# Retention heads and a cosine MLP on one core: the state product moved onto 64x64 quarters of the matmul array

## The chip, the cores and the metric

The kernel runs on one core of a Trainium2 chip. The metric is device time in microseconds (us) of that core, from launch to end; lower is better. The profile shows one execution, instruction by instruction, on the engines PE (matmul; PEld is its weight load), DVE (vector), ACT (scalar), POOL and SP (which only issues transfers).

## The reference

Two stages, one after the other. First a retention recurrence for 4 batches, 8 heads, 768 tokens and head size 64:

```
state = gamma[h] * state + outer(k[t], v[t])
y[t]  = scale * q[t] @ state
```

Then an MLP without bias over the 3072 tokens (model size 512, inner size 2048): `h = x @ w_in; out = (h * cos(h)) @ w_out`, where x is y with its heads side by side.

## The kernel before

**Chunks.** The recurrence is computed in chunks of 128 tokens. A slot is one chunk of two batches (b = 0 and 1), all 8 heads; 6 chunks and two pairs of batches make 12 slots, p = 0 to 11. In each slot PE makes, for each head and batch:

- A = k qᵀ inside the chunk (`a_mm`, L366): the 128 keys lie on PSUM partitions as two halves x = 0 and 1 of 64, and the 128 queries are columns. DVE multiplies A by a triangular mask into `am` (`a_mask`, L372).
- Y, in one PSUM bank for each batch, from three parts: the state times q (L428, in `y1_mm`), and `am` times v for each half of the keys (`intra`, L414). Keys of the second half see only queries of the second half, so there the matmul has 64 columns and not 128.
- S = kᵀ v, added to the running state in the bank `st_ps` (`s_mm`, L460): one matmul of 128 rows, 64 columns of the array and 64 moving columns for each head and batch. A copy of the state, `stb`, is used by the next slot.

The decay is folded into q and v by per-token factors (`gq`, `gk`; `conv_q`, `conv_v`). q and k reach PE transposed in `qkt`: by PE up to slot 5 (`t_mm`), by a DMA transpose from slot 6 on (`dma_t`, issued by SP).

**Quarters.** The 128x128 array can be used as four 64x64 quarters: a row group r (which 64 partitions feed it) and a column group c (which 64 PSUM partitions it writes). A and Y are written for quarters and S for halves of 128x64; everything else uses the whole array. Two row groups must not write one PSUM bank at the same time. Y's two halves of the keys sit on different row groups and go into the same bank, so `y1_mm` first sends each row group to its own bank, then `hop` puts a wait on another engine's queue (SP for p up to 5, POOL after), and `y2_mm` sends each row group to the other bank.

**The MLP** works on groups of two slots (512 tokens), g = 0 to 5: `f_mm` (L472, four matmuls of 512 columns for each of 16 blocks of the inner size), cosine by ACT (`f_cos`, L480), product by DVE (`f_mul`, L484), then `o_mm` (L517, 16 matmuls for each of 4 token blocks). Groups 0 and 1 can also be made in halves of 256 tokens (`h_mm`, L493); `HALF0` says for how many blocks of group 0.

**Order.** Up to slot 5 a planner (`Plan`) with a cost and a rank for every operation decides the order on each engine before the kernel is built; a seed and a jitter of the ranks pick one order among many. Where it finds PE without work early on it adds matmuls on zeros (`idle_mm`, L546). `LOADS` is the order of the big transfers on POOL's queue. From slot 6 on the order is written out: `block(p)` stands once in each 8 steps of the loop, each step being one `f_mm` and one quarter of an `o_mm`; in it stand Y's first part, the hop, A of slot p+1, Y's second part, the copies, and S. After it come the conversions of slot p+2, its two DMA transposes, and the loads of slot p+4, three transfers of 512 KB on SP's queue. The loads of slots 8 and 9 are issued just ahead of this loop.

**PSUM.** One bank of eight holds the state; the other seven go round among all users in the order in which they were given back.

Of the kernel before, what the change touches and what calls it, by code (L numbers as in the profile page):

```python
# [159 lines left out]
            op["fn"](op["eng"])  # L160


SEED, JIT, HOLD = 60, 4.0, "PD"
HALF0, SPARE, RF, RM, COLD = 4, 1, 40.0, 40.0, 5.2


@with_exitstack
def kernel(
# [21 lines left out]
    NB = 3  # L190
    DMA_T = 6

    ORDER = [0, NC] + [x for x in range(1, NP) if x != NC]
    LATE = NC

    scale = 1.0 / math.sqrt(D)
# [34 lines left out]
    cosb = [sb([128, 4 * C], BF16, f"cosb{i}") for i in range(3)]  # L231
    kx = sb([128, H, 2, D], BF16, "kx")
    vx = sb([128, 2, H, D], BF16, "vx")
    mask = sb([128, 128], BF16, "mask")
    zero = sb([128, 256], BF16, "zero")
    lgp = sb([128, NC, H], FP32, "lgp")
    gq = sb([128, NC, H], FP32, "gq")
    gk = sb([128, NC, H], FP32, "gk")


    gtf = gt[1].rearrange("p f t -> p (f t)")
# [23 lines left out]

    def load(eng, p, names):

        bp, c = divmod(ORDER[p], NC)
        for n in names.split():
            t, src = SRC[n[0].lower()]  # L270
            if len(n) == 1:
                t = (qb(p) if n == "Q" else kb(p)) if n in "QK" else t[p % PRE]
                eng.dma_start(  # L273
                    out=t.rearrange("p b h d -> p (b h) d"),
                    in_=src[ds(2 * bp, 2), :, ds(c * C, C), :].rearrange(
                        "b h t d -> t (b h) d"))
            else:
                b = int(n[1])
                eng.dma_start(
                    out=t[p % PRE][:, b],  # L280
                    in_=src[2 * bp + b, :, ds(c * C, C)].rearrange("h t d -> t h d"))
# [27 lines left out]
                             in1=bc(gq, ORDER[p] % NC), op=ALU.mult)  # L309

    def conv_v(p, b, e):
        ENG[e].tensor_tensor(out=vb(p)[:, b], in0=vf[p % PRE][:, b],  # L312
                             in1=bc(gk, ORDER[p] % NC), op=ALU.mult)

# [36 lines left out]
    def kt(n, b, h):  # L351
        return qkt[n][ts(b, 64), 1, h, :]

    def a_mm(p, u):
        n = p % NB
        bk = held["a", p, u] = [banks.take(), banks.take()]
        ap = [t.rearrange("p (a t) -> p a t", a=HP) for t in bk]
        for a in range(HP):
            h = 4 * u + a
            for x in range(1 if p < 2 else 2):  # L360
                for b in range(2):
                    if p < 2:
                        nc.tensor.matmul(ap[b][:, a, :], lhsT=kt(n, b, h), rhs=qt(n, b, h),  # L363
                                         tile_position=(64 * b, 0))
                        continue
                    nc.tensor.matmul(ap[b][ts(x, 64), a, :], lhsT=kt(n, b, h)[:, ts(x, 64)],  # L366
                                     rhs=qt(n, b, h), tile_position=(64 * b, 64 * x),
                                     skip_group_check=True)

    def a_mask(p, b, u):  # L370
        bank = held["a", p, u][b]
        nc.vector.tensor_tensor(  # L372
            out=am[p % 2][b][u], in0=bank.rearrange("p (a t) -> p a t", a=HP),
            in1=(dec[:, b] if p < 2 else mask.unsqueeze(1).to_broadcast([128, HP, 128])),
            op=ALU.mult)
        banks.give(bank)

# [28 lines left out]

    def intra(p, b, a, x, **kw):

        ms = []
        for j in range(2):
            h = 2 * a + j
            ms.append(nc.tensor.matmul(  # L414
                held["yp", p][b][ts(j, 64), a, 64 * x :], lhsT=vs[p % NB][ts(x, 64), b, h, :],
                rhs=am[p % 2][b][h // 4][ts(x, 64), h % 4, 64 * x :],
                start=False, stop=True, tile_position=(64 * x, 64 * j), skip_group_check=True))
        return ms

    def y1_mm(p):  # L420
        bk = [banks.take(), banks.take()]
        held["y", p, 0], held["y", p, 1] = bk
        held["yp", p] = [t.rearrange("p (a t) -> p a t", a=HP) for t in bk]
        for a in range(HP):
            for b in range(2):
                for j in range(2):
                    h = 2 * a + j
                    nc.tensor.matmul(  # L428
                        held["yp", p][b][ts(j, 64), a, :], lhsT=stb[p % 2][ts(b, 64), h, :],
                        rhs=qt(p % NB, b, h), start=(a == 0), stop=False,  # L430
                        tile_position=(64 * b, 64 * j), skip_group_check=True)
        for a in range(HP):
            held["part", p] = intra(p, 1, a, 1) + intra(p, 0, a, 0)

    def hop(p):
        ms = held["part", p]
        held["hop", p] = (nc.sync if p <= 5 else nc.gpsimd).nop(nofuse=True)
        for m in ms:
            after(m, held["hop", p])

    def y2_mm(p):
        for a in range(HP):
            for m in intra(p, 1, a, 0) + intra(p, 0, a, 1):
                if a == 0:
                    after(held["hop", p], m)

    def y_copy(p, b, e):
        bank = held["y", p, b]
        copy(e, xt[(p // 2) % 2][:, :, ts(2 * (p % 2) + b, C)],
             bank.rearrange("p (a t) -> p a t", a=HP))  # L450
        banks.give(bank)

    def has_s(p):
        return p != 1 and (p == LATE or ORDER[p] % NC < NC - 1)

    def s_mm(p):
        x = 1 if p == LATE else p
# [108 lines left out]
        in0=far[:, :8].unsqueeze(2).to_broadcast([128, 8, 16]),  # L566
        in1=far[:, 8:24].unsqueeze(1).to_broadcast([128, 8, 16]), op=ALU.add)
    nc.vector.tensor_scalar(out=ident, in0=dist, scalar1=0.0, scalar2=None, op0=ALU.is_equal)
    nc.vector.tensor_scalar(out=mask, in0=dist, scalar1=0.0, scalar2=None, op0=ALU.is_ge)
    nc.vector.tensor_scalar(out=far, in0=dist, scalar1=0.0, scalar2=1.0e6,  # L570
                            op0=ALU.is_lt, op1=ALU.mult)
    nc.vector.tensor_tensor(out=dist, in0=dist, in1=far, op=ALU.max)
# [9 lines left out]
    for i in range(7):  # L582
# [5 lines left out]
    MERGE = 4  # L588
    CQ, CD = "D", "P"
    SPLIT = {(1, 1, 0), (0, 1, 1)}  # L590
    HM, HCQ, HCV = "q2", "", ""
    plan = Plan({"bank": 7, "cos": 3, "sem": 8, "out": 4, "port": 1, "ring": 7}, 6.5)
    add = plan.add
    SB2 = {"D": (0.33, 0.42), "A": (0.49, 0.585)}
# [3 lines left out]
    prev = None  # L598
    at = lambda tm: dict(start=0.0, free=0.0, done=tm, lat=0.0)
    ld["q", 0, 0], ld["q", 0, 1], ld["k", 0, 0], ld["k", 0, 1] = map(at, (3.9, 5.0, 7.4, 7.4))  # L600
    LOADS = ["Q1", "K1", "v0", "v1", "w0a", "w0b", "w1", "w2", "q2", "k2", "w3a", "v2", "w3b", "o0", "q3", "k3", "v3",
             "o1", "o2", "o3", "q4", "k4", "v4", "q5", "k5", "v5", "q6", "k6", "v6",
             "q7", "k7", "v7"]
    LAG = {"w1": 0.15}
    pend = []
    for i, x in enumerate(LOADS):
# [25 lines left out]
    for p in range(PL + 2):  # L632
# [85 lines left out]
        if p < 2:  # L718
            for b in range(2):
                T["y", p, b] = add("E", 0.24, lambda e, p=p, b=b: y_first(p, b), ym[b], 10 * p + 3,  # L720
                                   [("bank", 1)], (), "col", name="y%d%d" % (p, b))
            if p == 0:
                T["s", p] = add("E", 0.25, lambda e, p=p: s_mm(p), sm, 17, (), (),
                                "col", name="s%d" % p)
        else:

            a_next = MERGE <= p < PL
            def y(e, p=p, a_next=a_next):
                y1_mm(p)
                hop(p)  # L730
                if a_next:
                    a_mm(p + 1, 0)
                    a_mm(p + 1, 1)
                    y2_mm(p)
                if has_s(p):
                    s_mm(p)
                if not a_next:
                    y2_mm(p)
            o = add("E", 0.66 + 0.445 * a_next + (0.35 if a_next else 0.45) * has_s(p), y,
                    ym[0] + ym[1] + sm, 10 * p + 3, [("bank", 6 if a_next else 2)], (), "quad",  # L740
                    name="y%d" % p)
            T["y", p, 0] = T["y", p, 1] = T["s", p] = o
            if a_next:
                T["a", p + 1, 0] = T["a", p + 1, 1] = o
# [56 lines left out]
    plan.run({"S": 2.5, "P": 3.2, "A": 5.5, "D": 3.6, "E": 4.2}, COLD, 0.6, (4.2, 18.0, 0.225, lambda e: idle_mm(e, 2)), HOLD)  # L801
    plan.emit()

    for p in (PL + 2, PL + 3):
        load(nc.sync, p, "q k v")


    def block(p):
        nxt = p + 1 < NP
        y1_mm(p)  # L810
        hop(p)
        if nxt:
            a_mm(p + 1, 0)
            a_mm(p + 1, 1)
        y2_mm(p)
        for b in range(2):
            y_copy(p, b, "A")
        if has_s(p):
            s_mm(p)
            s_copy(p, "D")  # L820
        if nxt:
            for u in range(2):
                for b in range(2):
                    a_mask(p + 1, b, u)
# [11 lines left out]
    for g in range(2, NG + 1):  # L836
        for s in range(16):
            hf, r = divmod(s, 8)
            p = 2 * (g + 1) + hf
            if g < NG:  # L840
                f_mm(g, s)
                f_cos(("f", g, s))
                f_mul(g, s)
            if g == NG and s == 12:
                last_o(NG - 1, 3)
                break
            o_mm(g - 1, *divmod(s, 4))
            if s % 4 == 3:
                o_out(g - 1, s // 4, "A")
            if p < NP and r == 3:  # L850
                block(p)
                if p + 2 < NP:
                    conv(p + 2)
                if p + 4 < NP:
                    load(nc.sync, p + 4, "q k v")
            if s % 4 == 3:
                o_dma(g - 1, s // 4)

# [29 lines left out]
```

## Time and profile before

| | |
|---|---|
| median of 3 runs | 209.99 us (209.96 to 210.13) |
| the profiled execution | 210.4 us, its span 208.5 us |
| PE busy | 203.3 us (97% of the span), 2017 matmuls |
| DVE, ACT, POOL busy | 107.8, 116.1, 80.1 us |
| granted PE clock | 1.0 throughout |
| bytes moved | 32.05 MB, mean 154 GB/s |

The span is the time from the first to the last instruction; 1.9 us of the execution lie outside it. In the page and its views an instruction is named by its line in the kernel, its engine and what it writes from what. A matmul's duration in these views includes its way through the array, so that neighbours overlap: what a matmul costs is read from the distance between starts.

### The profile page before, as it was taken

To read this page: it belongs to the slowest core of one execution; us is meant where nothing else is said; L and a number is where in the kernel's file an instruction comes from. 1 tells how busy PE (TensorE), PEld (TensorE's weight loads), DVE (VectorE), ACT (ScalarE), POOL (GpSimd) and SP (SyncE) were. 2 spreads that over 40 slices of the span, in tenths; PEclk is the share of its full clock that TensorE was granted. 3 is DMA by queue.
4 is the path that set the end of the run, shared out by engine and by line. 5 is a ranking of instruction groups with operands and counts; after the bars stand their busy time and mean duration, and the time that the engine had idled before them with its cause. 6 is when DMAs were issued, how large, how long until landed. Compare 5 with 4: busy or idle time off the path is not lost.

```text
span 208.5 us, 4822 instructions
## 1 busy us (share of the span) xinstructions
PE 203.3 (97%) x2017; PEld 108.9 (52%) x2017; DVE 107.8 (52%) x186; ACT 116.1 (56%) x194; POOL 80.1 (38%) x84
## 2 busy tenths in 40 slices
PE   7999999999999999999999999999999999999993
PEld 2556456889555545455455455454444444444462
DVE  4465888977725647438438438338332334443000
ACT  7777787579655456556556556554545553553120
POOL 8889979999999007007007007000000000000000
PEclk9999999999999999999999999999999999999999
DMA  6999999999999599999994602401101101110222
GB/s 117 183 260 222 309 251 293 209 331 343 343 296 185 149 237 247 211 209 239 227 237 47 176 0 54 150 0 57 50 0 53 50 9 44 50 50 21 80 79 76
DMA packets 57495, 32.05 MB, mean 154 GB/s; under 512 B 46592, under 2 KB 51968, under 8 KB 57472
## 3 DMA queue, kind: packets, MB, share of 16 engines
q0 software_dynamic: 14352, 15.47, 33.6%
q1 hardware_dynamic: 42976, 16.13, 32.0%
q8 instruction: 16, 0.26, 0.5%
q10 hardware_dynamic: 144, 0.13, 0.2%
q14 instruction: 7, 0.06, 0.1%
HBM read 27.26 MB, written 6.29 MB: 161 GB/s over the span
## 4 chain that ended last, share of the span: by engine, by line
PE 91%; DMA 6%; POOL 1%; DVE 0%; ACT 0%; issue 0%; DVEq 0%; POOLq 0%
PE bank L517 38%; PE bank L472 32%; PE bank L493 7%; DMA w_in_sb<-in_moe_w_in_dram 4%; PE bank L366 3%; PE bank L337 2%; PE bank L414 2%; PE st_ps L460 2%; PE bank L537 2%; PE bank L428 2%; DMA qf<-in_q_dram 1%; PE bank L546 1%; POOL am L384 1%; PE bank L363 0%; ACT gt L380 0%; DVE qs L299 0%
## 5 line engine op out<-in xcount | busy, mean ns | idle before, releaser
L480 ACT ACTIVATE cosb<-bank,halfpi 128x512 bf16<-128x512 f32 x96 | 65.6, 690 | 57.3 <-PE bank L472 52.7
L517 PE MATMUL bank<-w_out_sb,gt 128*128 128x512 bf16 x368 | 91.1, 379 | 0.0
L484 DVE TENSOR_TENSOR gt<-bank,cosb 128x512 bf16<-128x512 f32 x76 | 51.7, 689 | 55.3 <-ACT cosb L480 55.3
L472 PE MATMUL bank<-xt,w_in_sb 128*128 128x512 bf16 x304 | 77.0, 379 | 0.1
L517 PEld LDWEIGHTS <-gt 128*128 128x128 bf16 x368 | 35.6, 98 | 42.3
L472 PEld LDWEIGHTS <-w_in_sb 128*128 128x128 bf16 x304 | 28.9, 98 | 34.2 <-DMA w_in_sb<-in_moe_w_in_dram 0.4
L308 POOL TENSOR_TENSOR qs<-qf,gq 128x512 bf16<-128x512 f32 x18 | 18.5, 1045 | 44.8 <-PE bank L414 44.7
L372 DVE TENSOR_TENSOR am<-bank,mask 128x512 bf16<-128x512 f32 x40 | 24.8, 681 | 0.3 <-PE bank L366 0.3
L312 POOL TENSOR_TENSOR vs<-vf,gk 128x512 bf16<-128x512 f32 x22 | 22.7, 1045 | 1.6 <-DMA vf<-in_v_dram 1.4
L297 ACT COPY ob<-bank 128x512 f32<-128x512 f32 (+1 forms) x24 | 13.9, 578 | 15.4 <-PE bank L517 14.2
L493 PE MATMUL bank<-xt,w_in_sb 128*128 128x256 bf16 x160 | 18.8, 273 | 0.0
L297 ACT CAST xt<-bank 128x512 bf16<-128x512 f32 x24 | 12.9, 589 | 9.6 <-PE bank L414 9.0
L501 DVE TENSOR_TENSOR gt<-bank,cosb 128x512 bf16<-128x512 f32 x20 | 13.5, 689 | 8.8 <-ACT cosb L480 8.8
L493 PEld LDWEIGHTS <-w_in_sb 128*128 128x128 bf16 x160 | 15.4, 98 | 2.6
L299 DVE CAST stb<-st_ps 128x512 bf16<-128x512 f32 x10 | 6.9, 690 | 11.3 <-PE st_ps L460 11.1
L546 PE MATMUL bank<-zero 128*128 128x512 bf16 x33 | 10.6, 448 | 1.1 <-DVE halfpi L562 1.1
L297 ACT CAST ks<-kf 128x512 bf16<-128x512 f32 x20 | 11.5, 629 | 0.2 <-DMA kf<-in_k_dram 0.2
L273 POOL DMA_DIRECT2D vf<-in_v_dram x8 | 9.5, 1189 | 0.0
L297 ACT COPY qkt<-bank 128x512 bf16<-128x512 bf16 x13 | 7.1, 594 | 2.7 <-PE bank L337 2.4
L414 PE MATMUL bank<-am,vs 64*64 64x64 bf16 (+1 forms) x320 | 8.3, 205 | 0.1
L299 DVE COPY ob<-bank 128x256 f32<-128x256 f32 x1 | 0.4, 425 | 13.4 <-PE bank L537 13.4
L366 PE MATMUL bank<-qkt 64*64 64x128 bf16 x320 | 7.2, 218 | 0.0
(59 smaller groups left out, 108.8 us busy)
## 6 DMA issues: line engine op xcount, KB each, us to landing
out_dram<-ob SPq DMA_DIRECT2D x23, 256.0 KB, 2.3
vf<-in_v_dram POOLq DMA_DIRECT2D x8, 512.0 KB, 8.4
qf<-in_q_dram POOLq DMA_DIRECT2D x6, 512.0 KB, 10.4
kf<-in_k_dram POOLq DMA_DIRECT2D x6, 512.0 KB, 9.7
w_out_sb<-in_moe_w_out_dram POOLq DMA_DIRECT2D x4, 512.0 KB, 12.8
qf<-in_q_dram SPq DMA_DIRECT2D x4, 512.0 KB, 4.5
kf<-in_k_dram SPq DMA_DIRECT2D x4, 512.0 KB, 6.7
vf<-in_v_dram SPq DMA_DIRECT2D x4, 512.0 KB, 7.5
```

Of the source, the lines that this page charges most:

```text
L297: nc.scalar.copy(out=out, in_=in_)
L308: ENG[e].tensor_tensor(out=qb(p)[:, b], in0=qf[p % PRE][:, b], in1=bc(gq, ORDER[p] % NC), op=ALU.mult)
L312: ENG[e].tensor_tensor(out=vb(p)[:, b], in0=vf[p % PRE][:, b], in1=bc(gk, ORDER[p] % NC), op=ALU.mult)
L366: nc.tensor.matmul(ap[b][ts(x, 64), a, :], lhsT=kt(n, b, h)[:, ts(x, 64)], rhs=qt(n, b, h), tile_position=(64 * b, 64 * x), skip_group_che ...
L372: nc.vector.tensor_tensor(out=am[p % 2][b][u], in0=bank.rearrange("p (a t) -> p a t", a=HP), in1=(dec[:, b] if p < 2 else mask.unsqueeze(1 ...
L472: nc.tensor.matmul(bank, lhsT=w_in_sb[:, i, ts(f, 128)], rhs=xt[g % 2][:, i, :], start=(i == 0), stop=(i == KIN - 1))
L480: nc.scalar.activation(out=cb, in_=bank, func=AF.Sin, bias=halfpi)
L484: nc.vector.tensor_tensor(out=gt[g % 2][:, f, :], in0=bank, in1=cb, op=ALU.mult)
L493: nc.tensor.matmul(bank[:, ts(e, 256)], lhsT=w_in_sb[:, i, ts(f + e, 128)], rhs=xt[g % 2][:, i, ts(hf, 256)], start=(i == 0 and e == 0), s ...
L501: nc.vector.tensor_tensor(out=gt[g % 2][:, f : f + 2, ts(hf, 256)], in0=bank.rearrange("p (f t) -> p f t", f=2), in1=cb.rearrange("p (f t) ...
L517: nc.tensor.matmul(bank, lhsT=gt[g % 2][:, f, ts(j, 128)], rhs=w_out_sb[:, f, :], start=(f == 0), stop=(f == KOUT - 1))
L546: nc.tensor.matmul(bank[:, : 256 * n].rearrange("p (n t) -> p n t", n=n), lhsT=zero[:, :128], rhs=zero.unsqueeze(1).to_broadcast([128, n, ...
```

## The change

1. **S on quarters.** `s_part(p, r)` makes S from the 64 tokens of row group r: 32 matmuls of 64x64 for a slot where there were 16 of 128x64. Both row groups write the bank `st_ps`, so S too gets a hop between its two halves.
2. **One block.** `y_block` makes the lists of all matmuls of a slot for each row group (Y from the state, Y's first part, S's first half on row group 0, A of the next slot, Y's second part, S's second half on row group 1), and `quarters` emits them in one interleaved order, by a small table of when each quarter would be free. `told` places the two hops, on SP for p up to 4 and on POOL after. In slots 2 and 3 A of the next slot stays apart, as before.
3. **Halves swapped.** From slot 8 on (`SWAP`), for the four heads of one half (which half depends on the batch), the first 64 tokens of k and v lie on partitions 64 to 127 and the last 64 on 0 to 63. With that each quarter gets as many matmuls of 64 columns as of 128 in A and Y. It takes a second mask (two more small DVE instructions at the start), a factor table `gk3` with swapped copies (three small transfers on SP's queue after the planned part), and loads of k and v in six pieces each: 13 transfers for a slot instead of 3, with the same bytes in the same 256-byte runs.
4. A's matmul of the second half of the keys now has 64 columns and not 128 (`lo` in `a_one`), since its first 64 columns are masked away in any case.
5. **The planned part** gets another seed, other ranks for cosine and product, `HALF0` 6 for 4 (two more blocks of group 0 made in halves), another order of the loads of k3, v3 and o1, o2, and new costs for the Y blocks.

```diff
-SEED, JIT, HOLD = 60, 4.0, "PD"
-HALF0, SPARE, RF, RM, COLD = 4, 1, 40.0, 40.0, 5.2
+SEED, JIT, HOLD = 59011, 4.0, "PD"
+HALF0, SPARE, RF, RM, COLD = 6, 1, 50.0, 30.0, 5.2
...
+            elif n[1] == "s":
+                fl = t[p % PRE].rearrange("p b h d -> p (b h) d")
+                for x in range(2):
+                    for lo, n4, th in ((0, 4, x), (4, 8, 1 - x), (12, 4, x)):
+                        eng.dma_start(out=fl[ts(x, 64), ds(lo, n4), :],
...
+    def second(p, x, b, u):
+        return x ^ (u ^ b if p >= SWAP else 0)
...
+    def a_one(p, ap, u, a, b, x):
+        h, lo = 4 * u + a, 64 * second(p, x, b, u)
+        return nc.tensor.matmul(
+            ap[b][ts(x, 64), a, lo:], lhsT=kt(p % NB, b, h)[:, ts(x, 64)],
+            rhs=qt(p % NB, b, h)[:, lo:], tile_position=(64 * b, 64 * x), skip_group_check=True)
...
+    def quarters(rows):
+        free = [[0.0, 0.0], [0.0, 0.0]]
+        left = [list(r) for r in rows]
+        while left[0] or left[1]:
+            best = None
+            for r in range(2):
+                for c in range(2):
+                    nxt = next((m for m in left[r] if m[0] == c), None)
+                    if nxt:
+                        t = max(free[r][c], nxt[2])
+                        if best is None or t < best[0]:
+                            best = (t, r, nxt)
+            t, r, m = best
+            left[r].remove(m)
+            free[r][m[0]] = t + m[1] / 2.4
+            m[3]()
...
+    def s_part(p, r):
...
+                    m = nc.tensor.matmul(
+                        st_ps[ts(b, 64), h, :], lhsT=kb(x)[ts(r, 64), b, h, :],
+                        rhs=vb(x)[ts(r, 64), b, h, :],
+                        start=(ORDER[x] % NC == 0 and h == 0 and r == 0), stop=True,
+                        tile_position=(64 * r, 64 * b), skip_group_check=True)
+                    told("s", p, r, m)
...
+        for r in range(2):
+            ms = y_inter(p, r) + y_part(p, r, 0)
+            if has_s(p) and r == 0:
+                ms += s_part(p, 0)
+            if a_next:
+                ms += a_rows(p + 1, r)
+            ms += late(y_part(p, r, 1), t1)
+            if has_s(p) and r == 1:
+                ms += late(s_part(p, 1), t2)
+            rows.append(ms)
+        return quarters(rows)
...
+    for x in range(2):
+        nc.sync.dma_start(out=gk3[ts(x, 64), ds(n, n)], in_=gk3[ts(1 - x, 64), :n])
+    nc.sync.dma_start(out=gk3[:, ds(2 * n, n)], in_=gk3[:, :n])
     for p in (PL + 2, PL + 3):
-        load(nc.sync, p, "q k v")
+        load(nc.sync, p, "q ks vs")
...
     def block(p):
         nxt = p + 1 < NP
-        y1_mm(p)
-        hop(p)
-        if nxt:
-            a_mm(p + 1, 0)
-            a_mm(p + 1, 1)
-        y2_mm(p)
+        y_block(p, nxt)
         for b in range(2):
             y_copy(p, b, "A")
         if has_s(p):
-            s_mm(p)
             s_copy(p, "D")
```

## The prediction

> **What bounds the kernel now.** I read the page first: busy shares, then the chain that ended last.
>
> ```profile
> PE 203.3 (97%) x2017; PEld 108.9 (52%) x2017; DVE 107.8 (52%) x186; ACT 116.1 (56%) x194; POOL 80.1 (38%) x84
> PE 91%; DMA 6%; POOL 1%; DVE 0%; ACT 0%; issue 0%; DVEq 0%; POOLq 0%
> ```
>
> A busy PE is not by itself the bound, but the chain says it is: 91% of the span runs over PE, and no other engine is over 56% busy. The chain in order of time shows from where on:
>
> ```profile
> 11.08 8.57 DMA w_in_sb<-in_moe_w_in_dram
> 19.70 1.04 PE bank L472 x4
> ...
> 92.29 0.86 PE bank L517 x4
> 93.16 0.35 PE bank L428 x16
> ...
> 94.43 0.37 PE st_ps L460 x16
> 94.80 0.97 PE bank L472 x4
> 95.77 0.86 PE bank L517 x4
> ```
>
> PE's last wait for a transfer ends at 19.70 us (weights of the MLP). After it every piece is PE, back to back: four whole-array matmuls take 0.86 us, and 0.97 after a block of small ones. So what the change saves inside PE's blocks after 19.70 us comes off the end one for one, unless a new wait appears. Next, the timeline of PE over one such block (slot 7):
>
> ```profile
> 92.78 0.38 PE L517 MATMUL bank<-w_out_sb,gt 128*128 128x512 bf16 x1
> 93.08 0.42 PE L428 MATMUL bank<-qkt,stb 64*64 64x128 bf16 x16
> 93.33 0.33 PE L414 MATMUL bank<-am,vs 64*64 64x128 bf16 x14
> 93.46 0.22 PE L366 MATMUL bank<-qkt 64*64 64x128 bf16 x2
> 93.50 0.22 PE L414 MATMUL bank<-am,vs 64*64 64x128 bf16 x2
> 93.52 0.69 PE L366 MATMUL bank<-qkt 64*64 64x128 bf16 x30
> 94.00 0.42 PE L414 MATMUL bank<-am,vs 64*64 64x128 bf16 x16
> 94.36 0.44 PE L460 MATMUL st_ps<-vs,ks 128*64 128x64 bf16 x16
> 94.73 0.39 PE L472 MATMUL bank<-xt,w_in_sb 128*128 128x512 bf16 x1
> ```
>
> The first column is the start. From the first small matmul to the next whole-array one is 94.73 - 93.08 = 1.65 us. Read so, the blocks of slots 2 to 11 take 1.51, 1.28, 1.61, 1.62, then 1.65 five times, and 1.09 (slots 2 and 3 hold no A, slot 11 neither A nor S).
>
> **Prices, from the starts one by one in this window.** On one quarter matmuls of 128 columns start 56 ns apart (93.165, 93.221, 93.277), those of 64 columns 32 ns apart (94.409, 94.441, 94.473); four quarters run side by side, starts 3 to 4 ns apart. Going from whole array to quarters costs 0.09 us (the last L517 starts at 92.776, plus its 0.216), the way back 0.10, and quarters to S's halves 0.09 again (the last L414 matmul, 94.211 plus 0.056, to 94.357). A hop costs 0.33: in slot 11, where nothing hides it, Y's first part has its last start at 155.766 and the second its first at 156.093.
>
> **S on quarters.** Removed: one change of tiling, 0.09. The S matmuls themselves gain nothing: 8 to a column group at 32 ns = 0.26 before, 8 to each quarter at 32 ns = 0.26 after; what can be gained is that they fill quarters that stand idle in Y and A. One row speaks for that, S's own 32-ns pitch with 64 columns, since twice as many matmuls are issued. The Trainium skill speaks against it ("TensorEngine Tiling (Array Packing)", Instruction Overhead): a matmul has some 60 cycles of overhead, and a tiling factor should not be taken from a dimension that is already small. Read per quarter that would be 25 ns, under the 32 measured; read as a cost on one issue path it would make 112 matmuls 2.8 us, which the 3-ns starts contradict.
>
> **The blocks after**, from the load of the fullest quarter, plus 0.015 for the slow first matmul and 0.10 for the way back:
> - Slots 4 to 6, row group 0, column group 0: 4 (state) + 8 (Y) + 8 (A) of 128 columns and 8 of 64 (S): 20 x 56 + 8 x 32 = 1.38, so 1.49. A's shorter second half lies on other quarters and gives nothing here. Saved: 0.12, 0.13, 0.16.
> - Slot 7 (A of slot 8 is the first with swapped halves): 16 x 56 + 12 x 32 = 1.28, so 1.40; saved 0.25.
> - Slots 8 to 10, all quarters equal: 12 x 56 + 16 x 32 = 1.18, so 1.30; saved 0.35 each, 1.05.
> - Slots 2 and 3, no A to fill the hop of S: S's first half on row group 0 has its last start at 8 x 56 + 7 x 32 = 0.67, plus the hop 0.33 = 1.00, plus 8 x 32 for the second = 1.26, so 1.37. Slot 2 saves 0.14 (0.2 of its present 1.51 is a wait for the mask on DVE, which now has a group of 0.86 more in front); slot 3 loses 0.09.
> - Slot 11: last start 0.37, hop 0.33, then 0.18: 0.87, so 0.99; saved 0.10.
>
> Sum: 0.14 - 0.09 + 0.41 + 0.25 + 1.05 + 0.10 = 1.86 saved.
>
> **What goes off that.** The emitted order is one list made with 53 and 27 ns where the rows say 56 and 32. If PE starts matmuls strictly in that order, stepping through it with the measured pitches gives 1.42, 1.31 and 1.23 for 1.38, 1.28 and 1.18: 0.3 over seven blocks. If quarters run apart, nothing. The timeline above shows two of A (93.46) starting before two of Y (93.50) that stand ahead of them in the program, so I am nearer to nothing and take 0.15. The skill ("TensorE: Matmul & The Clock Gate", Part 3, The mechanism) says that matmuls start and end strictly in program order; by that the full 0.3 would count. A of slot 2 is now in two pieces with a group between: two more changes of tiling, 0.2, against 0.15 of waiting in its present 0.72 (the same A takes 0.57 in slot 3): 0.05. Two blocks of L472 at 0.86 become two pairs in halves at 8 x 0.109: 0.02. Left: 1.65 saved.
>
> **Costed at nothing, and the cover.** The two mask instructions: DVE is idle 0.86 us just after, waiting for q. The hops: an event on SP or POOL takes 17 ns; in the program nothing waits ahead of them in slots 2 to 4, and from slot 5 they stand on POOL behind conversions that end over 10 us earlier in the loop ("POOL qs L308 <- PE bank L414" in the waits is POOL idle at this very spot, 44.7 us in 4). In slot 5 the cover is thin: a 1.05-us conversion just ahead ends perhaps 1 us early; if late, it costs that. The second hop holds up only conversions for two slots on. Before 19.70 us the order on PE is the same, with the same 33 matmuls on zeros, so PE meets the same weights at the same time. Slot 6's transposes now have the two hops of slot 4 ahead of them on SP, and slot 5's block is nearer: they landed 1 us before that block, I count 0 to 0.3 and take 0.
>
> The loads: SP has 29 issues for slots 8 and 9 where it had 6, and slot 8's transposes queue behind:
>
> ```profile
> 71.77 0.39 SPq L273 DMA_DIRECT2D qf<-in_q_dram  x1
> 80.89 2.97 SPq L273 DMA_DIRECT2D vf<-in_v_dram  x1
> 84.03 2.54 SPq L326 DMA_TRANSPOSE qkt<-ks  x1
> 86.68 1.24 SPq L326 DMA_TRANSPOSE qkt<-qs  x1
> ```
>
> An unhindered issue takes 0.35 to 0.39, so 29 need 10 us, under the 12.1 that the six take now because the transfers themselves are full. The last transpose lands at 89.6 (86.68 + the 2.9 of the page); A of slot 8 starts at 93.46, about 1 us earlier after the change. That leaves 2.5 to 3 us for slower small transfers: 0 to 1 us, taken as 0.
>
> **Forecast.** The profiled execution took 210.4 (span 208.5), 0.4 above the median; 210.4 - 1.65 = 208.75 there, and 208.4 for the median.
>
> **Rivals.**
> 1. Slower: PE is not fed fast enough. The fastest stretch of 64 small matmuls now (62.13 to 62.92) takes 12.4 ns each, and the whole of Y and A in slot 7, 80 matmuls in 1.18 us, 14.8. Slots 8 to 10 need 10.6. At 14.8 a block of 112 is 1.66 + 0.11 = 1.77, seven of them lose 0.9, with the rest 0.8: 210.8. It decides above 13.6 ns, where such a block equals the present mean of 1.64. For it: no long stretch faster than 12.4 is on the trace. Against: even that one follows its quarters' loads, and 16 in a row came at 10.4. At just 12.4 the block is 1.50 and the time 208.9 to 209.0.
> 2. A part lost to waits: slot 8's transposes late, or the new planned order leaves PE idle somewhere between 20 and 70 us, where now it never is. Up to 1 us: 208.9 to 209.5. The skill ("DMA: Bandwidth & Descriptors", Rules for kernel authors) advises against many small transfers and against splitting by partition halves, since both use the same engines; no transfer of 64 partitions is on this trace.
> 3. More gained: quarters run quite apart and no order is lost: 1.8, so 208.2.
> 4. Nothing gained, where S's second half waits out its hop in every block: 0.3 x 7 goes off, 210.1.
>
> **How the numbers follow.** About 0.2% (0.4 us) is what can be told from no change. Chances: forecast and rival 3 0.58, rival 2 and the 12.4-ns case 0.20, rival 4 0.08, rival 1 0.14. So faster 0.78, same 0.08, slower 0.14. The range from 207.9 to 209.6 holds the first two groups.
>
> **What would show it.** After: blocks of slots 8 to 10 from first small matmul to next whole-array one 1.25 to 1.40; slots 4 to 6 about 1.5; slot 3 longer than 1.28; no L460-like line between quarters and whole array; the 0.86 pieces unchanged. Wrong if starts inside the blocks are evenly 13 ns or more apart (rival 1), or if PE shows idle time before A of slot 8 or in the planned part (rival 2).

## The result: 218.02 us, 3.8% slower

The changed kernel takes 218.02 us (median of 4 runs, 217.42 to 218.56) beside 209.98 for the kernel before: ratio 1.0382, 95% interval 1.0346 to 1.0417. The forecast was 208.4 with a range to 209.6. The profiled execution took 217.57 us with a span of 215.8. The page of the kernel after, its busy shares and the chain that ended last:

```profile
PE 202.0 (94%) x2144; PEld 110.2 (51%) x2169; DVE 111.1 (51%) x187; ACT 116.5 (54%) x195; POOL 80.6 (37%) x84
PE 76%; SPq 10%; DMA 5%; DVE 3%; issue 2%; POOL 2%; ACT 1%; POOLq 0%; ACTq 0%; DVEq 0%
```

PE's busy time is nearly the same, 202.0 us beside 203.3. (The page is short by at least 25 matmul records, 2144 beside 2169 weight loads, so the small difference says nothing; two blocks read long for that reason and are left out below.) The chain is what changed: SP's queue, which was not on it, now holds 10% of it, and PE only 76% where it had 91%. The same chain in order of time shows where SP comes in:

```profile
73.45 1.35 SPq L910
...
95.11 0.63 SPq L285
95.90 1.28 SPq L346
97.29 2.75 DMA qkt<-qs
100.18 0.39 PE bank L385 x5
```

From 73.45 to 97.29 us the end of the kernel hangs on nothing but SP issuing (SPq is SP's queue): three copies of gk (L910, L911), 26 loads (L277, L285), then slot 8's transposes (L346). PE's timeline over the same block that the prediction showed (slot 7, which makes A of slot 8), and two lines of slot 9's block:

```profile
94.69 0.42 PE L490 MATMUL bank<-qkt,stb 64*64 64x128 bf16 x16
94.94 0.33 PE L476 MATMUL bank<-am,vs 64*64 64x128 bf16 x14
100.18 0.32 PE L385 MATMUL bank<-qkt 64*64 64x64 bf16 x2 [4.91 <-DMA qkt<-qs]
...
132.38 0.42 PE L490 MATMUL bank<-qkt,stb 64*64 64x128 bf16 x16
...
133.73 1.04 PE L586 MATMUL bank<-xt,w_in_sb 128*128 128x512 bf16 x3
```

Y's first part starts at 94.69, and then PE stands still for 4.91 us until `qkt` of slot 8 lands. Slot 9's block, which waits for nothing, goes from 132.38 to 133.73: 1.34 us by the exact starts, close to the forecast 1.30; it took 1.65 before. And this is SP's queue, to be read against the four lines of before (there six loads, from 71.77 to 83.86, then the transposes):

```profile
76.17 0.54 SPq L277 DMA_DIRECT2D qf<-in_q_dram  x1
76.82 4.69 SPq L285 DMA_DIRECT2D kf<-in_k_dram  x6
81.60 4.46 SPq L285 DMA_DIRECT2D vf<-in_v_dram  x6
...
95.90 1.28 SPq L346 DMA_TRANSPOSE qkt<-ks  x1
97.29 1.24 SPq L346 DMA_TRANSPOSE qkt<-qs  x1
```

13 issues take 9.9 us. In the chain the single pieces mostly read 0.61 to 0.64 us, the 64 KB ones like the 128 KB ones, and the first of a group of six 1.1 to 1.3 in three of the four groups. The loss goes on after the wait. Windows of 2 to 5 us around it (busy time of each engine, then the granted clock, the DMA share and GB/s):

```profile
95.00:100.00 5.00, 0.27 (x22) 0.12 (x11) 0.35 (x1) 0.38 (x1) 0.00 (x0) 0.77 0.72 163
100.00:102.00 2.00, 1.82 (x83) 1.68 (x84) 0.02 (x1) 0.59 (x1) 0.74 (x1) 0.50 0.88 202
102.00:104.00 2.00, 1.78 (x4) 0.67 (x6) 2.00 (x4) 1.76 (x4) 2.00 (x3) 0.50 0.97 217
```

PE's granted clock falls to 0.50 while PE still waits (0.77 is the mean of the first window), and stays there for some 4 us of its work. The rest of the block then takes 2.33 us and the next two groups 3.01 instead of 1.73. The transfers were not full: a DMA share of 0.72 at 163 GB/s in the wait, 0.65 at 154 GB/s from 70 to 94 us, against 0.91 at 207 there before.

Laid out by place (start of each block in both traces):

| stretch | before, us | after, us | difference |
|---|---|---|---|
| start to slot 2's transposes | 27.10 | 28.57 | +1.47 |
| to slot 6's block | 50.42 | 50.69 | +0.27 |
| to slot 7's block | 15.56 | 15.43 | -0.13 |
| to slot 8's block | 15.57 | 22.44 | +6.87 |
| to slot 11's block | 46.70 | 45.77 | -0.93 |
| to the end | 53.19 | 52.90 | -0.29 |

The +6.87 is 4.91 of waiting, 0.90 and 1.28 at half clock, less 0.22 that the block saves. In the last row the block of slot 11 saves 0.07, and the last store lands some 0.2 sooner after its copy. The +1.47 comes from the start of the kernel. DVE's and ACT's timelines there:

```profile
1.81 1.00 DVE L685 TENSOR_SCALAR mask<-gt 64x128 bf16<-64x128 f32 x2
```

```profile
3.42 2.45 ACT L694 ACTIVATE gt<-gt,lnsc 128x128 f32<-128x128 f32 x8 [1.40 <-DVE gt L689]
```

The second mask's two instructions (211 and 779 ns) stand on DVE ahead of `dist`, so ACT's exponentials start at 3.42 instead of 2.39 us. But the chain that ended last does not run over the mask here. At its start it runs over the landing of v and over a cast of v on DVE, on which PE waits before it begins the MLP. First the cast's line before, then after, then the chain of after:

```profile
14.58 0.44 DVE L299 CAST gt<-vf 128x512 bf16<-128x512 f32 x1
```

```profile
15.18 1.87 DVE L311 CAST gt<-vf 128x512 bf16<-128x512 f32 x1
```

```profile
5.14 7.62 DMA vf<-in_v_dram
12.78 0.69 DVE gt L311
13.47 1.79 DVE am L404 x3
15.25 1.80 DVE gt L311
17.10 0.41 PE bank L427 x8
17.51 0.98 PE bank L607 x8
```

The cast took 1.87 us where it took 0.44 before. PE's first matmul on the MLP's weights (17.45 by its exact start; 15.68 before) comes 0.40 us after the end of this cast in all eleven traces of kernels with the new planned order, and the cast takes from 0.75 to 2.4 us in them. So two things delay the start, the mask and this cast.

### The profile page after: what moved, and what is told of

It is laid out like the page before. It is cut to its first block, busy times and chain, and to the rows that moved or that the text cites. A ratio compares the mean times of both kernels' runs of the same rounds, so it can differ in the third digit from the quotient of the medians.

```text
span 215.8 us, 5170 instructions
## 1 busy us (share of the span) xinstructions
PE 202.0 (94%) x2144; PEld 110.2 (51%) x2169; DVE 111.1 (51%) x187; ACT 116.5 (54%) x195; POOL 80.6 (37%) x84
## 4 chain that ended last, share of the span: by engine, by line
PE 76%; SPq 10%; DMA 5%; DVE 3%; issue 2%; POOL 2%; ACT 1%; POOLq 0%; ACTq 0%; DVEq 0%
PE bank L631 31%; PE bank L586 25%; PE bank L607 9%; SPq L285 8%; DMA vf<-in_v_dram 4%; PE bank L385 2%; PE bank L476 2%; PE bank L357 2%; PE bank L651 2%; PE bank L490 1%; DMA qkt<-qs 1%; DVE gt L311 1%; PE st_ps L504 1%; SPq L910 1%; DVE am L404 1%
## 5 line engine op out<-in xcount | busy, mean ns | idle before, releaser
L586 PE MATMUL bank<-xt,w_in_sb 128*128 128x512 bf16 x282 | 73.7, 382 | 0.7 <-issue 0.4
L586 PEld LDWEIGHTS <-w_in_sb 128*128 128x128 bf16 x296 | 28.4, 98 | 33.6 <-issue 0.7
L607 PE MATMUL bank<-xt,w_in_sb 128*128 128x256 bf16 x176 | 20.5, 273 | 0.4 <-DVE gt L598 0.3
L607 PEld LDWEIGHTS <-w_in_sb 128*128 128x128 bf16 x176 | 17.0, 98 | 3.5 <-issue 0.6
L332 POOL TENSOR_TENSOR vs<-vf,gk 128x512 bf16<-128x512 f32 x14 | 14.6, 1049 | 3.4 <-PE st_ps L504 3.2
L385 PE MATMUL bank<-qkt 64*64 64x64 bf16 (+1 forms) x320 | 8.8, 213 | 4.9 <-DMA qkt<-qs 4.9
L476 PE MATMUL bank<-am,vs 64*64 64x128 bf16 (+1 forms) x320 | 10.6, 209 | 0.1
L385 PEld LDWEIGHTS <-qkt 64*64 64x64 bf16 x320 | 7.4, 112 | 6.3 <-issue 5.5
L277 POOL DMA_DIRECT2D vf<-in_v_dram x8 | 9.4, 1172 | 0.1
```

What stands on the lines that cost most here:

```text
L385: return nc.tensor.matmul(ap[b][ts(x, 64), a, lo:], lhsT=kt(p % NB, b, h)[:, ts(x, 64)], rhs=qt(p % NB, b, h)[:, lo:], tile_position=(64 * ...
L476: m = nc.tensor.matmul(held["yp", p][b][ts(j, 64), a, lo:], lhsT=vs[p % NB][ts(r, 64), b, h, :], rhs=am[p % 2][b][h // 4][ts(r, 64), h % 4 ...
L586: nc.tensor.matmul(bank, lhsT=w_in_sb[:, i, ts(f, 128)], rhs=xt[g % 2][:, i, :], start=(i == 0), stop=(i == KIN - 1))
L607: nc.tensor.matmul(bank[:, ts(e, 256)], lhsT=w_in_sb[:, i, ts(f + e, 128)], rhs=xt[g % 2][:, i, ts(hf, 256)], start=(i == 0 and e == 0), s ...
```

## The experiments

Theory 1: the number of issues on SP ahead of slot 8's transposes costs the 6.9 us. Theory 2: the second mask's place costs some 1 us at the start. Rivals: the swap itself, transfers of 64 partitions, or the new planned order. The ratios below are to the kernel before, run beside each group of runs (medians of 210.31, 210.36 and 210.26).

**No swap, loads whole.** SWAP beyond the last slot, k and v one load each, no copies of gk; the second mask is still built.

```diff
-    SWAP = 8
+    SWAP = 99
-        load(nc.sync, p, "q ks vs")
+        load(nc.sync, p, "q k v")
```

> The changed kernel without swapped halves: k and v of slots 8 to 11 are loaded by one transfer each, no factor copies; S stays on quarters in one block. Theory 1 (SP needs about 0.63 us for each piece, so that 29 issues take 22 us and the transposes of slot 8 come too late): PE's wait of 4.9 us in slot 7 and its slow clock after it (1.3 us) go, slots 7 to 10 cost 1.51 us instead of 1.34, about 0.6 more in all: 211.8 us. Rival (S on quarters or the one block is what costs the time): it stays above 217.

210.65 us (210.62 to 211.44), ratio 1.0028 [1.0013, 1.0044]. The wait is gone, every block of slots 6 to 10 takes 1.517, slot 11 1.090. The time is 1.15 under the expected one: the start lost 0.77 less here (slot 2's transposes at 27.80, where the changed kernel has 28.57), and the slow clock that went with the wait had cost 2.18 us and not the 1.3 counted.

**No swap, six pieces.** The same without the swap, but with loads cut in six as in the change.

```diff
-                    for lo, n4, th in ((0, 4, x), (4, 8, 1 - x), (12, 4, x)):
+                    for lo, n4, th in ((0, 4, x), (4, 8, x), (12, 4, x)):
```

> The changed kernel with k and v loaded in six pieces each, but no halves swapped (each piece goes where it would have gone in one transfer). Theory 1: the wait in slot 7 is there as in the changed kernel, and the blocks are 0.6 us longer in all: 218.6 us. Rival (the swapped data, its mask or its factors cause the wait): 211.8 us, as without pieces.

218.57 us, ratio 1.0388 [1.0339, 1.0436]: the whole loss is back without any swap. PE waits 4.6 us in slot 7, its clock is 0.79 from 94 to 110 us as in the changed kernel. The wait in this run:

```profile
PE bank L385 <- DMA qkt<-qs: 4.6, 1, 4.6
```

**No swap, two pieces.** All 16 pairs of batch and head of one half of the partitions in one transfer.

```diff
+                for x in range(2):
+                    eng.dma_start(out=fl[ts(x, 64)], in_=src[ds(2 * bp, 2), :, ds(c * C + 64 * x, 64), :]
+                                  .rearrange("b h t d -> t (b h) d"))
```

> As the run before, but k and v in two pieces each, of 64 partitions and all 16 heads: the same bytes, all in transfers of 64 partitions, 10 issues for slots 8 and 9 and not 26. Theory 1 (the number of issues decides): SP is through with them in 7 to 12 us, as before the change; no wait in slot 7; 211.8 us. Rival (transfers of 64 partitions move slowly): the transposes come late all the same, over 216 us.

210.49 us, ratio 1.0017 [1.0004, 1.0031]. Transfers of 64 partitions do no harm by themselves; it is how many there are. One such issue of 256 KB took 0.8 to 2.7 us and not 0.63, so the price is not free of size above 128 KB: with the copies of gk, 13 issues kept SP 14.6 us ahead of slot 8's transposes, where 7 to 12 was expected.

**The mask later, first try.** The changed kernel with the second mask's two instructions after the factors `lgp`, and with `dist` and `far` exchanged so that the raw distances stay.

> The changed kernel with the two instructions of the second mask moved behind the decay exponents' inputs on DVE (after the eight of L691). Theory 2 (the second of them takes 0.78 us where DVE prepares the decay, ACT's exponents start 1.03 us later, and the first MLP matmuls 1.8): the transposes of slot 2 start at 27.1 us as in the kernel before and not at 28.6; 216.5 us. Rival (the new planned order itself is slower in the first 30 us): 218.0 us, as the changed kernel.

217.89 us, ratio 1.0339 [1.0283, 1.0394], but it says nothing on theory 2: with this exchange ACT's first wait came ahead of its table load (at 2.43 instead of 0.74 us), so the exponentials began at 3.73 and not at 2.4. Two runs below take theory 2 up again.

**Swap kept, four pieces.** Two transfers of 128 partitions for the heads that stay in place, two of 64 for those that are swapped.

```diff
+                for lo in (0, 12):
+                    eng.dma_start(out=fl[:, ds(lo, 4), :], in_=whole[:, ds(lo, 4), :])
+                for x in range(2):
+                    eng.dma_start(out=fl[ts(x, 64), ds(4, 8), :], in_=whole[ts(1 - x, 64), ds(4, 8), :])
```

> The change with its swap kept, but with k and v of a slot in four transfers each (two of 128 partitions by 4 pairs of batch and head, two of 64 partitions by 8) instead of six: 9 issues for a slot instead of 13. Theory (SP's time for each small load, 0.6 to 0.66 us, puts slot 8's transposes behind 22 us of issues): from 73.45 us SP needs 2.5 us for the copies of gk and 2 x (0.55 + 8 x 0.62) = 11.0 for the loads, the transposes are issued at 87 to 89 us, PE does not wait in slot 7, whose block is 1.4 us; slots 8 to 10 take 1.34. Against the run without swap (210.65, blocks 1.517 and 1.090) that saves 0.12 + 3 x 0.175 + 0.07 = 0.7: 209.9, give or take the 0.8 by which the start varies. Rival (transfers that land on swapped halves are late by themselves, or transfers of 64 partitions are): PE still waits 3 us or more in slot 7, over 213.

210.56 us, ratio 1.0008 [0.9996, 1.002]. No wait; blocks of 1.430 in slot 7, 1.342 in slots 8 to 10, 1.020 in slot 11, and 0.85 us less from slot 2's transposes to the end than with whole loads and no swap (180.23 against 181.08). The price of an issue was again too low in the expectation: from 73.61 to 90.70 SP needed 17.1 us and not 13.5, so the transposes began at 90.70 and not at 87 to 89, only just in time.

**Six pieces, one slot later.** All 13 issues of a slot stay, but slot 9's stand behind slot 8's transposes, and so on.

```diff
-    for p in (PL + 2, PL + 3):
-        load(nc.sync, p, "q ks vs")
+    load(nc.sync, PL + 2, "q ks vs")
...
-                if p + 4 < NP:
-                    load(nc.sync, p + 4, "q ks vs")
+                if p + 3 < NP:
+                    load(nc.sync, p + 3, "q ks vs")
```

> The change with all six pieces, but slot 9's loads are issued after slot 8's transposes instead of ahead of them, and each later slot's one slot later as well: 13 issues and the three copies stand ahead of slot 8's transposes instead of 29. Theory (a burst of issues ahead of the transposes, while 13 issues of 0.65 = 8.5 us fit into a slot's 15.5): transposes issued at 86 to 89 us, no wait of PE in slots 7 to 10, blocks 1.4, 1.34 three times, time 209.9 give or take 0.8. Rival (the pieces are too slow at any time): waits of PE on the transposes in slots 7 to 10, over 213.

210.07 us, ratio 0.9995 [0.9981, 1.0009]. SP's queue in this run:

```profile
76.15 0.54 SPq L277 DMA_DIRECT2D qf<-in_q_dram  x1
76.78 4.97 SPq L285 DMA_DIRECT2D kf<-in_k_dram  x6
81.85 4.82 SPq L285 DMA_DIRECT2D vf<-in_v_dram  x6
86.83 1.26 SPq L346 DMA_TRANSPOSE qkt<-ks  x1
```

The pieces cost just as much, but the transposes start at 86.83 instead of 95.90, and PE waits for no transfer in slots 7 to 10. So the pieces fit into a slot; what hurt was two slots of them in a row ahead of the transposes. Theory 1 stands, its rivals fall.

Side by side, from SP's first issue after the planned part to slot 8's first transpose:

| loads | issues | SP, us | PE's wait in slot 7, us |
|---|---|---|---|
| whole | 6 | 11.8 | none |
| two pieces | 13 | 14.6 | none |
| six pieces, one slot later | 16 | 13.2 | none |
| four pieces | 21 | 17.1 | none |
| four pieces, the mask late (below) | 21 | 18.0 | 0.58 |
| six pieces, no swap | 29 | 22.1 | 4.6 |
| the change | 29 | 22.4 | 4.9 |

**No swap, no second mask.** As the first run, and the mask's two instructions left out (nothing reads them there).

> No swap (every slot as slots 4 to 6), k and v one load each, no copies of gk, and the second mask is not built either: only S on quarters, the block in one order and the new planned order are left of the change. Theory (the second mask's two instructions on DVE, 1.0 us, push the exponentials and all of PE's first work): against the run of the same kernel with the mask (210.65) the exponentials start at 2.4 instead of 3.4 us, the first matmul on the weights at 15.7 to 16.2 instead of 16.68, time 209.6 to 210.1. Rival (the new planned order itself starts late): the weights start at 16.7 as before and the time stays within 210.4 to 210.9.

210.24 us, ratio 0.9993 [0.9977, 1.0008]. The exponentials start at 2.39, the weights at 16.42, slot 2's transposes at 27.55. The cast of v took 1.87 us in this trace as in the changed kernel's, where the transposes stand at 28.57: 1.02 us for the mask, the microsecond by which the exponentials moved. But the median fell by only 0.41 against the first run, between theory and rival; in that run's trace the cast took 1.54 and the transposes stand at 27.80. So it is shown that the mask moves the exponentials by 1.03 us. What of that reaches the end is not settled: 0.4 by the medians, 0.25 to 1.0 by the traces. The chain of the first run does go over the mask (2.03 to 2.81) and the exponentials, that of the changed kernel over v's landing and the cast. The rest of the 1.47 (27.55 against 27.10 before) goes with the length of the cast: in two traces below with the new order and no early mask, in which it took 0.75 and 0.77, the transposes stand at 26.70 and 26.61.

**Four pieces, the mask late.** The raw distances get a tile of their own, and the second mask is built after the planned part.

> The four transfers for k and v with swap, and the second mask built on DVE after the planned part, from a tile of its own that keeps the raw distances. If both theories hold, the exponentials start at 2.4 us, PE has no wait in slot 7, and the time is 0.5 to 1.0 under that of the four transfers alone: 208.9 to 209.4, faster than the kernel before by 0.3 to 0.5%. If the early loss is the planned order's, it equals the four transfers alone, 209.9.

210.06 us (208.85 to 210.86), ratio 0.9986 [0.9969, 1.0002]. The exponentials start at 2.4, and the mask's two instructions, now at 73 us with POOL idle, took 0.21 and 0.22 us. Slot 2's transposes stand at 28.01, with 0.4 us of waiting for the MLP's weights ahead of them. PE came to slot 7's block 0.6 us earlier than in the run with four pieces, and waited there 0.58 us for slot 8's `qkt`: that cover was used up, and the block took 2.218, 0.79 more than without a wait. With it the time missed the expected 208.9 to 209.4.

**S after the block, on whole arrays.** As the run without second mask, with `quarters` for Y and A only, and S as 16 matmuls of 128 rows behind them.

> No swap, plain loads, no second mask as in the run at 210.24, but S is taken off the quarters again: Y and the next A are still planned over the quarters, and S follows on whole arrays as 16 matmuls. By the prediction's prices a block of slots 4 to 10 is then 20 x 56 + 0.015 ns-start + 0.09 change of tiling + 8 x 32 + 0.09 = about 1.6 us against 1.517 with S on quarters, and slots 2 and 3 fall from 1.353 to about 1.28: together 7 x 0.1 - 2 x 0.07 = +0.5 us, so 210.7. Rival (S on quarters is worth nothing, all of the swap-free gain is the order of Y and A): blocks of 1.52 again and 210.2.

211.67 us, ratio 1.0057 [1.0038, 1.0076]: blocks of 1.62 and 1.63 in slots 4 and 5, 1.709 in slots 6 to 10 and 1.446 in slots 2 and 3. So S on quarters is worth 0.115 us a block in slots 4 and 5, about the 0.1 expected, and 0.19 in slots 6 to 10. Slots 2 and 3 went the other way than expected (0.09 longer, not 0.07 shorter), probably because nothing fills Y's hop when S stands behind it. Together that is 1.4 us, the difference of the two medians (211.67 and 210.24).

**All mends together.** Four pieces, loads one slot later, the mask late.

> Everything that the runs point to, with swap: four transfers for each of k and v, loads one slot later (slot 9's behind slot 8's transposes), the second mask built after the planned part. Against the four transfers with the late mask (span 209.0 with a wait of 0.88 in slot 7's block, 2.218 instead of 1.342 to 1.40) that wait goes: about 0.8 less, 209.2 (208.9 to 209.6), faster than the kernel before. Rival: if the start or something else takes the 0.8 back, 210.0.

209.50 us (208.51 to 210.37), ratio 0.9959 [0.9938, 0.9979]: 0.4% faster than the kernel before. The wait in slot 7 is gone, its block takes 1.430.

**The old planned order.** As the run without second mask, with the old seed, ranks, `HALF0` and order of loads; PE's groups then stand as before.

```diff
-SEED, JIT, HOLD = 59011, 4.0, "PD"
-HALF0, SPARE, RF, RM, COLD = 6, 1, 50.0, 30.0, 5.2
+SEED, JIT, HOLD = 60, 4.0, "PD"
+HALF0, SPARE, RF, RM, COLD = 4, 1, 40.0, 40.0, 5.2
```

> No swap, plain loads, no second mask, and the planned part made with the old parameters (seed, how many half groups, ranks, order of the loads): PE's groups then stand in exactly the order of the kernel before, with the new blocks in place of the old. Theory (the new planned order itself costs about 0.55 us between slot 2's transposes and slot 6: a change of tiling more for A of slot 2, and PE idle 0.36 near 36.5 us until a multiplication on DVE): that stretch falls from 50.70 to 50.13 us, no wait on DVE near 36.5, and the time is 209.7. Rival (the order is worth nothing): 50.7 and 210.2.

209.45 us, ratio 0.9957 [0.9944, 0.9971]. In the changed kernel PE waits in the planned part:

```profile
37.50 4.53 PE L607 MATMUL bank<-xt,w_in_sb 128*128 128x256 bf16 x40 [0.34 <-DVE gt L598]
```

With the old order this wait is gone, but slot 2's block waits for its mask again (1.580 against 1.353), as before. So the stretch from slot 2's transposes to slot 6 falls from 50.71 to 50.39, 0.32 where 0.55 was expected. The median falls by more, 0.79. The rest must lie ahead of slot 2's transposes, where a single trace tells little (27.55 and 27.22 here, but 26.61 to 28.01 over the traces with the new order and no early mask); with the old order the cast of v took 0.41 to 0.44 us in every trace.

**All mends and the old order.**

> As the version with four transfers, loads one slot later and the late mask, but with the old planned order. If the old order is worth 0.55 us, this takes 0.55 less than that version: 208.7 (208.3 to 209.2), some 1.5 us faster than the kernel before in the same call. If not, the two agree.

208.74 us (208.34 to 209.18) against 210.26 for the kernel before, ratio 0.9929 [0.9912, 0.9946]. The change's idea is worth 1.5 us once its loads, its mask and its planned order are put right, close to the 1.6 that the prediction had forecast for the change as it stood. About half of it is the swap: the run before, with the same order and no swap, gains 0.8. Against the version with the new order the gain is 0.76 and not 0.55. Its chain that ended last:

```profile
PE 96%; DMA 1%; ACT 1%; DVE 0%; issue 0%; DVEq 0%; POOLq 0%
```

## Why the prediction was wrong

- **Blocks: right.** Predicted 1.37 (slots 2, 3), 1.49 (4 to 6), 1.40 (7), 1.30 (8 to 10), 0.99 (11), plus 0.15 over all for the order. Measured, in blocks without a wait: 1.353, 1.50 to 1.52 (in the run without swap and mask), 1.430 (with four pieces), 1.342, 1.019. Summed over the slots they save 1.63, where the prediction had 1.86 less 0.15. The pitches of 56 and 32 ns held, and the rival in which PE is not fed fast enough did not occur: 112 matmuls in 1.34 us are 12 ns each.
- **The loads: wrong, and this decided it.** The step "an unhindered issue takes 0.35 to 0.39, so 29 need 10 us" took its price from one whole load of q into an empty queue and from stores, though the same trace has two later loads of q at 0.53 and 0.54. The pieces took 0.61 to 0.64 and up to 1.3 for the first of a group, q itself 0.54: 22.3 us for 29, 0.77 each. What the step needed was the point from which it turns. PE was ready for A at 95.27; from the first transpose's issue to the second's landing it took 4.14 (95.90 to 100.04); so the loads had to be issued by 91.1, and from 73.45 that leaves 0.61 us an issue. The trace of before held no issue of this kind, and its other six were 2.0 us in the mean (12.1 / 6). A price taken from one end of 0.39 to 2.0, with the turn at 0.61 between them, could not be "0 to 1 us, taken as 0".
- **The rival "a part lost to waits" had the place and not the size.** It named slot 8's transposes, with a bound of 1 us; they cost 4.91 of waiting and 2.2 more at half clock, a term that the prediction does not have. The wait was not bounded by what one transfer is late: it was the backlog of the queue. The advice against many small transfers in the Trainium skill ("DMA: Bandwidth & Descriptors", Rules for kernel authors), which the prediction cited there, agrees with the run in two pieces against that in six (210.49 and 218.57). Its advice against splitting by partition halves has as its reason that both halves use the same engines; that is not what bound here. Halves alone cost nothing (210.49, and 210.65 with whole loads), and in the changed kernel the DMA share was only 0.65 while SP was issuing without a pause.
- **The mask, costed at nothing: it moved the exponentials by 1.03 us, and the time by 0.4 between the medians.** "DVE is idle 0.86 us just after" was true and beside the point: what stands behind the two instructions is `dist`, on which ACT's exponentials wait. And the two took 1.0 us together, not the 0.43 that they take where they stand late.
- **The planned order: 0.05 and 0.02 for what cost 0.57.** From slot 2's transposes to slot 6 the run without swap and mask needs 50.71 where before needs 50.42, though its four blocks there save 0.29. Some 0.35 is the wait on DVE near 37 us, which the rival of lost waits had as "PE idle somewhere between 20 and 70 us"; the rest is put down to A of slot 2 in two pieces, which no run took apart. And "PE meets the same weights at the same time" did not hold: the order on PE was the same, but PE waited for the cast of v (17.45 for 15.68 in the changed kernel, mask included).
- **Hops, slot 5's POOL queue, slot 6's transposes: nothing, as forecast.** Slots 5 and 6 take 1.517 in the run without swap and mask. In other runs they read up to 1.62, with a pause of some 0.1 ahead of a matmul of S; no run says why.

## What to carry to other kernels

A transfer has a price on the queue that issues it, and a change that cuts loads into pieces must be costed there: pieces times the price of one such issue, measured at the same size and with the queue as full, up to the first instruction behind them on which another engine waits, and with the price at which that wait begins written beside it. Ask of every instruction added ahead of a chain not whether its engine has idle time, but what stands behind it in program order. A good idea and a bad schedule add up to one number: here 1.5 us gained and over 8 lost, and only one run for each part told them apart.

## What the runs showed of the hardware

- The price of a small load on SP's queue, where nothing holds it up, depended little on its size: 0.61 to 0.64 us for 64 partitions with 64 or 128 KB, 0.51 to 0.57 for 128 partitions with 128 KB, 0.54 for q's 512 KB into an empty queue. The first of a group often took 1 us or more.
- Some 2.5 us into the 4.9 without work PE's granted clock fell to half, and it stayed there for about 4 us after work began again; after the wait of 0.58 us in the run with four pieces and the late mask it kept 1.00. The slow clock added 2.18 us to the 4.91 of the wait.
- Two kinds of DVE instruction took longer than usual, some of them until an issue on POOL ended. The second mask instruction took 0.78 us and ended at 2.81, as POOL's issue of a transfer ended (2.79); built late, with POOL idle, it took 0.22. The cast of v took 0.41 to 0.44 us in the kernels with the old order and 0.75 to 2.4 in those with the new one; in the changed kernel (15.18 to 17.05) it ended 0.24 after an issue of POOL that began while the cast was under way (15.61 to 16.81). That the two share something is only argued from these ends and stays open: other DVE instructions beside the same issue on POOL took their usual 0.22 and 0.29, and in the run with all mends the cast began before such an issue (14.72 to 15.92) and ended inside it, after 0.77. It may go with the spread of these kernels' times: the one-slot-later kernel's twelve runs lie at 209.8 to 210.1 and at 210.6 to 210.9.
